# Later weight conversions, a sum's guard on ScalarE, four score buffers and transposes two slots behind, in an attention and two-layer-block kernel

## The chip, the cores and the metric

The kernel runs on one core of a Trainium2 chip. The metric is device time in microseconds (us) for one execution, median of three runs. The engines are named as in the profile: PE is TensorE (PEld its weight loads), DVE is VectorE, ACT is ScalarE, POOL is GpSimd, SP is SyncE, which issues all DMAs here.

## What is computed

The reference chains three parts. Inputs are float32 activations and weights drawn in float64.

```python
scores = scale * q @ k.T + decay           # decay from cumulated log f, causal mask
attn = exp(scores - max); attn = attn / (attn.sum() + 1e-9)
x = (attn @ v)  as (2304 tokens, 512)      # 4 batches x 8 heads, 576 tokens, head size 64
h = x @ w_in;  g = h * tanh(softplus(h));  y = g @ w_out      # 512 -> 2048 -> 512
a = y @ w1; b = y @ w2; out = ((a * b) @ w3) @ w_out2         # 512 -> 1024 -> 1024 -> 512
```

The weights w_in, w_out, w1, w2, w3 and w_out2 come as float64 bit patterns and are converted to float32 on the chip. Nearly every product is made of three matmuls over a high and a low part of its operands (float32r), so each tensor is split into two tiles.

## The kernel before, in words

The program has two phases. Phase A holds attention for 16 pairs of heads, all weight conversions, the product of w3 and w_out2 (`wp_unit`), and the first layer (`l1_all`) for batches 0 to 2. Phase B holds the first layer of batch 3 and then everything behind it, in eight blocks of 288 tokens.

Attention is cut into units. A unit is 128 rows of one head's scores; a pair of heads has 9 units, of which the last (number 8 of the pair) takes the 64 remaining rows of both heads and reads all 576 columns. There are 144 units. The loop in `phase_a` has a slot for each unit and seven more. In slot s it writes out, in program text:

- `scores(s)`: two to eight matmuls on PE into one of two PSUM banks, ps_s (L391, L392, L401);
- `softmax_a(s)`: masking and row minimum on DVE into a buffer P (L415; L417 and L418 for a pair's last unit), then the exponential on ACT in place, with the row sum (L419);
- `transposes(s - T_LAG)`: up to five PE transposes of P into ps_t, two PSUM banks (L455), a copy of the high part to `pt` on ACT (L483) and a subtraction for the low part on DVE (L485);
- `inv_sums` on a pair's last slot: 1e-9 is added to nine row sums (L426), and the reciprocal is taken (L427), both on DVE. `inv_rows` transposes it (L434, L436) and stores it to DRAM, `inv_load` reads it back broadcast as R, and `x_parts` multiplies by it (L521);
- `pv` in two slots of each pair: attention times v into ps_v (L503), then `x_rows` on ACT and DVE (L515, L516), `x_parts` on POOL and ACT;
- filler: matmuls of `wp_unit` (L550) or of the first layer (L580), a planned number for each slot.

A conversion is a DMA of 512 KB (L111) into one of two buffers `cvr`, a scaling on POOL (L124; for other weights on ACT, L126) and three bit operations on DVE (L134, L135, L136). For w_out (tiles `cvu`, 16 of them) and for w1 and w2 (tiles `cvv`, 16) the result is stored to DRAM (L143) for phase B. The loop places job i of these 32 in slot `W_OUT_SLOT + int(W_OUT_STEP * i)`.

The program's text does not fix the order on an engine. A scheduler gives each engine its instructions by priority and by its own model of when each could run; the score, transpose and subtraction steps have a raised priority, the conversions do not. Each engine then runs its list in that order.

Of the kernel before, what the change touches and what calls it, by code (L numbers as in the profile page):

```python
# [8 lines left out]
F32 = mybir.dt.float32  # L9
# [3 lines left out]
AF = mybir.ActivationFunctionType  # L13
ALU = mybir.AluOpType
# [4 lines left out]
B, H, S, D = 4, 8, 576, 64  # L19
# [11 lines left out]
PT_N = 1536  # L31

QK_AT = ((-2, 4, 5, 5, 6), (3, 9, 9, 10, 11))
T_LAG = 1
PV_AT = (3, 5)
HB = 3
CV = 2
# [6 lines left out]
MID = 7  # L44
EARLY = 10
W3_STEP = 2.25
W_OUT_STEP = 2.25
PRE = 6
WP_END = 51
W_IN_SLOT = 34  # L50
W_IN_STEP = 1.25
W_OUT_SLOT = 62
L1_S = (42, 75, 114, 153)

MM_PAIRS = ((0, 0), (0, 1), (1, 0))
# [12 lines left out]
class Kernel:  # L68
# [116 lines left out]
    def att_pool(self):  # L185
        nc = self.nc
        self.attp = self.tc.tile_pool(name="att", bufs=1)
        a = self.att = self.attp.__enter__()
        self.psp = self.tc.tile_pool(name="psa", bufs=1, space=PSUM)
        p = self.psp.__enter__()  # L190
        self.ps_s = [p.tile([128, 512], F32, name=f"ps_s{i}") for i in range(2)]
        self.ps_t = [p.tile([128, 512], F32, name=f"ps_t{i}") for i in range(2)]
        self.ps_v = p.tile([128, 1024], F32, name="ps_v")
        self.ident = a.tile([128, 128], F32, name="ident")
        self.m1 = a.tile([128, 512], BF16, name="m1")
        self.m4 = a.tile([128, TB], BF16, name="m4")
        self.pt = a.tile([128, 6 * PT_N + 3 * 64], F32R, name="pt")
        self.pt4 = self.pt[:, 6 * PT_N:]
        self.TT = [a.tile([128, 2, 1216], F32R, name=f"T{i}") for i in range(3)]
        self.T = [(t[:, 0], t[:, 1]) for t in self.TT]  # L200
        self.P = [a.tile([128, n], F32, name=f"P{i}") for i, n in enumerate((512, 512, S))]


    def decay_log(self):
# [67 lines left out]
    def zeros(self):  # L272

        nc = self.nc
        z = self.m1[:, :384]
        nc.gpsimd.memset(self.P[2][0:4], 1.0)
        for i in (0, 2, 1):
# [8 lines left out]
            for c in (d0, d0 + S):  # L286
                nc.scalar.copy(t2[0:4, c:c + S], self.P[2][0:4])

# [115 lines left out]
    def softmax_a(self, u):  # L404
        _, _, c = self.unit(u)
        nc = self.nc
        n = S if c == 4 else 128 * (c + 1)
        P = self.P[u % 3]
        i = (0, 1, 2, 3, 5, 6, 7, 8, 4)[u % 9]
        if u % 9 == 0:  # L410
            self.sums = self.att.tile([128, 16], F32, name=f"sum{u // 9}", tag="sum", bufs=2)
        st = self.sums[:, 9 + u % 3:10 + u % 3]
        ttr = nc.vector.tensor_tensor_reduce
        if c < 4:
            ttr(P[:, :n], self.ps_s[u % 9 % 2][:, :n], self.m1[:, 512 - n:], -0.125, 3.0e38, ALU.add, ALU.min, st)  # L415
        else:
            ttr(P[:, :TB], self.ps_s[0][:, :TB], self.m1[:, :TB], -0.125, 3.0e38, ALU.add, ALU.min, self.sums[:, 12:13])  # L417
            ttr(P[:, TB:n], self.ps_s[1][:, :TB], self.m4, -0.125, self.sums[:, 12:13], ALU.add, ALU.min, st)  # L418
        nc.scalar.activation(P[:, :n], P[:, :n], AF.Exp, bias=st, scale=-1.0,  # L419
                             accum_out=self.sums[:, i:i + 1])  # L420

    def inv_sums(self):

        nc = self.nc
        r = self.sums[:, 0:9]
        nc.vector.tensor_scalar(r, r, 1e-9, None, ALU.add)  # L426
        nc.vector.reciprocal(r, r)  # L427
        self.inv = r

# [18 lines left out]

    def transposes(self, u):
        _, _, c = self.unit(u)  # L450
        P = self.P[u % 3]
        for kc in range(c + 1):
            o = 128 * (kc % 4)
            k = 64 if kc == 4 else 128
            self.nc.tensor.transpose(self.t_bank(u, kc)[0:k, o:o + 128], P[:, 128 * kc:128 * kc + k], self.ident)  # L455
# [190 lines left out]
    def phase_a(self):  # L646
# [48 lines left out]
        def job(s, key, src, fin, *a):  # L695
            at(s, self.cv_load, key, src)
            conv.setdefault(s + 1, []).append(key)
            at(s + 2, fin, *a)
# [7 lines left out]
        for i in range(32):  # L706
# [3 lines left out]
            else:  # L710
                key, src, dst = f"v{f}", self.cols((self.w1, self.w2)[f % 2], f // 2), self.w12_scr
            job(W_OUT_SLOT + int(W_OUT_STEP * i), key, src, self.cv_store, key, dst[f])
        for p in range(NPAIR):
# [21 lines left out]
        for s in range(nslot + 7):  # L735
# [3 lines left out]
            with self.tc.high_priority(offset=HP_ATT):  # L739
                if s < nslot:  # L740
                    self.scores(s)
                if 0 <= s - T_LAG < nslot:
                    self.transposes(s - T_LAG)
                    self.pt_parts(s - T_LAG, False)
            for key in conv.get(s, []):
# [5 lines left out]
            self.run_filler(k)  # L751
            if 0 <= s - T_LAG < nslot:
                with self.tc.high_priority(offset=HP_ATT):
                    self.pt_parts(s - T_LAG, True)
            for key in conv.get(s, []):
# [287 lines left out]
```

## Time and profile before

| quantity | value |
|---|---|
| median of 3 runs | 1089.82 us (1088.87 to 1092.64) |
| the profiled execution's own time | 1095.71 us |
| its span, first to last instruction | 1094.0 us |
| PE busy | 980.8 us, 90% |
| DVE, ACT, POOL busy | 788.5, 639.1, 592.7 us |
| mean granted TensorE clock | 0.954 of full speed |

The span is the time between the first and the last instruction of one profiled execution; a busy share is an average over both phases. The last score unit's exponential starts at 488.0 us, and phase B's first matmuls follow at about 505 us. The granted clock has two levels, 1.2 and 2.4 GHz, shown as 0.50 and 1.00 where a stretch has one level alone.

### The profile page before, as it was taken

To read this page: it belongs to the slowest core of one execution; us is meant where nothing else is said; L and a number is where in the kernel's file an instruction comes from. 1 tells how busy PE (TensorE), PEld (TensorE's weight loads), DVE (VectorE), ACT (ScalarE), POOL (GpSimd) and SP (SyncE) were. 2 spreads that over 40 slices of the span, in tenths; PEclk is the share of its full clock that TensorE was granted. 3 is DMA by queue.
4 is the path that set the end of the run, shared out by engine and by line. 5 is a ranking of instruction groups with operands and counts; after the bars stand their busy time and mean duration, and the time that the engine had idled before them with its cause. 6 is when DMAs were issued, how large, how long until landed. Compare 5 with 4: busy or idle time off the path is not lost. (4 is left out here: it accounts for less than half of the span.)

```text
span 1094.0 us, 20534 instructions
## 1 busy us (share of the span) xinstructions
PE 980.8 (90%) x6784; PEld 935.2 (85%) x6784; DVE 788.5 (72%) x1800; ACT 639.1 (58%) x1660; POOL 592.7 (54%) x690
## 2 busy tenths in 40 slices
PE   0797778888789888998979999999999999999998
PEld 0576657788789878998878999999999999999998
DVE  7977788785666776643897886868868687886821
ACT  7676778876665677764666454545545454454511
POOL 5956677775666677623685453534545353453500
PEclk9898869899889998998999999999999999999999
DMA  7865457667667867425864111121111112111100
GB/s 212 207 209 173 131 164 219 195 183 222 199 201 229 249 203 219 150 72 170 298 188 126 39 44 45 44 61 39 50 45 44 50 44 61 39 50 40 27 23 22
DMA packets 107086, 136.37 MB, mean 125 GB/s; under 512 B 11092, under 2 KB 83172, under 8 KB 106980
## 3 DMA queue, kind: packets, MB, share of 16 engines
q1 hardware_dynamic: 106980, 135.07, 41.7%
q8 instruction: 53, 0.87, 0.3%
q14 instruction: 53, 0.43, 0.1%
HBM read 98.39 MB, written 36.54 MB: 123 GB/s over the span
## 5 line engine op out<-in xcount | busy, mean ns | idle before, releaser
L580 PE MATMUL ps_l<-x,wi 128*128 128x288 f32 x1536 | 250.6, 312 | 14.5 <-ACT x L88 4.1
L580 PEld LDWEIGHTS ps_l<-x,wi 128*128 128x128 f32 x1536 | 224.7, 198 | 20.5 <-ACT hst L587 5.2
L889 PE MATMUL ps_x<-g,wo 128*128 128x288 f32 x1536 | 224.5, 297 | 6.8 <-POOL g L102 3.7
L889 PEld LDWEIGHTS ps_x<-g,wo 128*128 128x128 f32 x1536 | 209.6, 189 | 11.0 <-POOL g L102 6.0
L102 POOL TENSOR_TENSOR g<-mb,g 128x288 fp32r<-128x288 f32 x128 | 111.5, 871 | 135.5 <-ACT g L88 130.7
L102 POOL TENSOR_TENSOR T<-raw,T 64x288 fp32r<-64x288 f32 x128 | 113.3, 904 | 16.9 <-ACT T L339 11.9
L88 ACT CAST g<-mb 128x288 fp32r<-128x288 f32 x128 | 55.3, 432 | 112.8 <-DVE mb L853 82.5
L830 ACT ACTIVATE ma<-ma 128x288 f32<-128x288 f32 x128 | 56.6, 442 | 101.9 <-DVE ma L826 101.9
L908 PE MATMUL ps_y<-x,w 128*128 128x288 f32 x768 | 108.2, 296 | 2.6 <-ACT x L897 1.3
L908 PE MATMUL ps_l<-x,w 128*128 128x288 f32 x768 | 108.1, 295 | 0.0
L908 PEld LDWEIGHTS ps_y<-x,w 128*128 128x128 f32 x768 | 104.0, 189 | 3.0 <-ACT x L897 1.5
L908 PEld LDWEIGHTS ps_l<-x,w 128*128 128x128 f32 x768 | 104.3, 189 | 0.0
L455 PE MATMUL ps_t<-ident,P 128*128 128x128 f32 (+1 forms) x400 | 73.0, 301 | 32.9 <-DVE pt L485 32.5
L419 ACT ACTIVATE P<-P,sum 128x512 f32<-128x512 f32 (+2 forms) x144 | 85.4, 595 | 27.8 <-DVE sum L415 24.9
L485 DVE TENSOR_TENSOR pt<-ps_t,pt 128x128 fp32r<-128x128 f32 (+2 forms) x288 | 83.2, 331 | 24.6 <-ACT pt L483 24.1
L834 DVE SCALAR_TENSOR_TENSOR mb<-ma 128x288 f32<-128x288 f32 x128 | 63.3, 494 | 51.0 <-POOL g L102 49.2
L849 POOL TENSOR_TENSOR mb<-mb,hl 128x288 f32<-128x288 f32 x64 | 63.4, 991 | 62.7 <-DVE cs L847 29.3
L849 POOL TENSOR_TENSOR mb<-mb,hsp 128x288 f32<-128x288 f32 x64 | 61.8, 965 | 64.1 <-issue 25.7
L483 ACT CAST pt<-ps_t 128x128 fp32r<-128x128 f32 (+2 forms) x288 | 73.0, 314 | 34.5 <-PE ps_t L455 32.6
L848 DVE SCALAR_TENSOR_TENSOR ma<-cs,ma 128x288 f32<-128x288 f32 x128 | 89.5, 699 | 2.4
L455 PEld LDWEIGHTS ps_t<-ident,P 128*128 128x128 f32 (+1 forms) x400 | 52.3, 152 | 41.9 <-DVE pt L485 34.0
L847 DVE SCALAR_TENSOR_TENSOR cs<-mb,ma 128x288 f32<-128x288 f32 x128 | 73.6, 575 | 13.4 <-ACT ma L839 12.6
(123 smaller groups left out, 1917.7 us busy)
## 6 DMA issues: line engine op xcount, KB each, us to landing
raw<-in_qk_dram SPq DMA_DIRECT2D x64, 288.0 KB
h_scr<-h SPq DMA_DIRECT2D x96, 144.0 KB
hl<-h_scr SPq DMA_DIRECT2D x64, 144.0 KB
hsp<-h_scr SPq DMA_DIRECT2D x64, 144.0 KB
cvrt<-in_w3t_dram SPq DMA_DIRECT2D x16, 512.0 KB
cvri<-in_w_in_dram SPq DMA_DIRECT2D x16, 512.0 KB
cvru<-in_w_out_dram SPq DMA_DIRECT2D x16, 512.0 KB
cvrv<-in_w_dram SPq DMA_DIRECT2D x16, 512.0 KB
```

Source lines behind the costliest of these rows:

```text
L102: self.nc.gpsimd.tensor_tensor(lo[..., c], raw[..., c], f32(hi[..., c]), ALU.subtract)
L419: nc.scalar.activation(P[:, :n], P[:, :n], AF.Exp, bias=st, scale=-1.0, accum_out=self.sums[:, i:i + 1])
L455: self.nc.tensor.transpose(self.t_bank(u, kc)[0:k, o:o + 128], P[:, 128 * kc:128 * kc + k], self.ident)
L483: nc.scalar.copy(hi, a)
L485: nc.vector.tensor_tensor(self.pt_dst(hd, 1, k, 128 * c, w), a, f32(hi), ALU.subtract)
L580: mm(o[:, :TB], w, x, start=i == 0, stop=i == 11)
L834: self.nc.vector.scalar_tensor_tensor(b, a, 2.0, a, ALU.add, ALU.mult)
L847: nc.vector.scalar_tensor_tensor(e, b, 2.0, a, ALU.add, ALU.mult)
L848: nc.vector.scalar_tensor_tensor(a, e, 2.0, a, ALU.subtract, ALU.mult)
L849: nc.gpsimd.tensor_tensor(b, b, self.hl[c], ALU.mult)
L889: mm(self.xb(e), self.wo[f][:, 512 * a + 128 * e:512 * a + 128 * e + 128], g[:, TB * b:TB * b + TB], start=f == 0 and k == 0, stop=f == 15 ...
L908: mm(ps, self.w12[f, i][:, 512 * a + 128 * e:512 * a + 128 * e + 128], self.x2[e][:, TB * b:TB * b + TB], start=n == 0, stop=n == 11)
```

## The change

Five edits. `T_LAG` goes from 1 to 2, so a unit is transposed two slots behind its scores. There are four P buffers, each 576 columns wide, in place of three of 512, 512 and 576. The 32 conversion jobs of w_out, w1 and w2 are placed from slot 88 in steps of 1.9 slots, in place of slot 62 and 2.25. The addition of 1e-9 is an ACT instruction.

```diff
-T_LAG = 1
+T_LAG = 2
...
-W_OUT_STEP = 2.25
+W_OUT_STEP = 1.9
...
-W_OUT_SLOT = 62
+W_OUT_SLOT = 88
...
-        self.P = [a.tile([128, n], F32, name=f"P{i}") for i, n in enumerate((512, 512, S))]
+        self.P = [a.tile([128, S], F32, name=f"P{i}") for i in range(4)]
...
-        P = self.P[u % 3]
+        P = self.P[u % 4]
...
-        nc.vector.tensor_scalar(r, r, 1e-9, None, ALU.add)
+        nc.scalar.activation(r, r, AF.Copy, bias=1e-9)
         nc.vector.reciprocal(r, r)
```

What the scheduler makes of it is seen in the order of instructions. Three places follow.

The first place is DVE, the last of the 32 conversions (`cvv15`). `sum14` and `sum15` are the row sums of pairs 14 and 15 (units 126 to 134 and 135 to 143), and L415 is the row-minimum step of a unit. Before:

```order
L415 ISA P0_92,sum14_4750<-ps_s1_81,m1_86 128x512
L415 ISA sum14_4750 128x1
L134 TENSOR_SCALAR cvv15_4966<-cvv15_4966 128x512
L485 TENSOR_TENSOR pt_88<-ps_t1_83,pt_88 128x128
L135 SCALAR_TENSOR_TENSOR cvv15_4966<-cvrv15_4932,cvv15_4966 128x512
L136 SCALAR_TENSOR_TENSOR cvv15_4966<-cvrv15_4932,cvv15_4966 128x512
```

Of the change:

```order
L415 ISA P3_95,sum15_4996<-ps_s0_80,m1_86 128x128
L415 ISA sum15_4996 128x1
L485 TENSOR_TENSOR pt_88<-ps_t1_83,pt_88 128x128
L134 TENSOR_SCALAR cvv15_5415<-cvv15_5415 128x512
L135 SCALAR_TENSOR_TENSOR cvv15_5415<-cvrv15_5397,cvv15_5415 128x512
L485 TENSOR_TENSOR pt_88<-ps_t0_82,pt_88 64x64 x2
L136 SCALAR_TENSOR_TENSOR cvv15_5415<-cvrv15_5397,cvv15_5415 128x512
```

The last conversion moved from behind the row minimum of unit 129 to behind that of unit 139. The first one (`cvu0`) stands behind that of unit 59 before and of unit 58 in the change, although its slot number is 26 higher.

The second place is DVE at the end of pair 9. The rows `128x2x64 x4` and `64x64 x2` are the six subtractions of the pair's last unit, number 89; `sum10` belongs to the next pair. Before:

```order
L427 RECIPROCAL sum9_3067<-sum9_3067 128x9
L485 TENSOR_TENSOR pt_88<-ps_t0_82,pt_88 128x2x128 x2
L415 ISA P2_94,sum10_3407<-ps_s0_80,m1_86 128x384
L415 ISA sum10_3407 128x1
L485 TENSOR_TENSOR pt_88<-ps_t1_83,pt_88 128x2x64 x4
L485 TENSOR_TENSOR pt_88<-ps_t0_82,pt_88 64x64 x2
L134 TENSOR_SCALAR cvu15_3629<-cvu15_3629 128x512
```

Of the change:

```order
L415 ISA P1_93,sum10_3295<-ps_s1_81,m1_86 128x512
L415 ISA sum10_3295 128x1
L485 TENSOR_TENSOR pt_88<-ps_t1_83,pt_88 128x2x64 x4
L415 ISA P2_94,sum10_3295<-ps_s0_80,m1_86 128x128
L415 ISA sum10_3295 128x1
L485 TENSOR_TENSOR pt_88<-ps_t1_83,pt_88 128x128
L134 TENSOR_SCALAR cvu13_4177<-cvu13_4177 128x512
L485 TENSOR_TENSOR pt_88<-ps_t0_82,pt_88 64x64 x2
```

The row minima run one unit further ahead of unit 89's subtractions, and a conversion's first step now stands ahead of the last two of them.

The third place is PE at the end of phase A. L434 transposes the last pair's reciprocals, L503 is `pv`, and the tiles x12 to x15 are inputs of the first layer for batch 3 (x15 belongs to the last pair). Before:

```order
L434 MATMUL ps_t0_82<-ident_85,sum15_5072 9x128
L580 MATMUL ps_l1_65<-x14_0_5246,wi0_1343 128x288 x2
L580 MATMUL ps_l0_64<-x12_1_4627,wi0_1343 128x288 x3
L580 MATMUL ps_l0_64<-x13_1_4958,wi0_1343 128x288 x3
L580 MATMUL ps_l0_64<-x14_1_5250,wi0_1343 128x288 x3
L503 MATMUL ps_v_84<-pt_88,V15_5296 128x256 x2
L503 MATMUL ps_v_84<-pt_88,V15_5296 128x128 x2
L503 MATMUL ps_v_84<-pt_88,V15_5296 128x320 x6
L503 MATMUL ps_v_84<-pt_88,V15_5296 128x192 x2
L503 MATMUL ps_v_84<-pt_88,V15_5296 128x64
L580 MATMUL ps_l1_65<-x15_0_5487,wi0_1343 128x288
```

Of the change, from L434 on:

```order
L434 MATMUL ps_t0_82<-ident_85,sum15_4996 9x128
L503 MATMUL ps_v_84<-pt_88,V15_5262 128x320 x5
L503 MATMUL ps_v_84<-pt_88,V15_5262 128x192 x2
L580 MATMUL ps_l1_65<-x8_1_3179,wi12_1932 128x288 x3
L580 MATMUL ps_l1_65<-x9_1_3520,wi12_1932 128x288 x3
L580 MATMUL ps_l1_65<-x10_1_3863,wi12_1932 128x288 x3
```

And of the change, around the last `pv`:

```order
L503 MATMUL ps_v_84<-pt_88,V15_5262 128x320 x6
L503 MATMUL ps_v_84<-pt_88,V15_5262 128x192 x2
L503 MATMUL ps_v_84<-pt_88,V15_5262 128x64
L580 MATMUL ps_l0_64<-x12_1_4544,wi0_1327 128x288 x3
L580 MATMUL ps_l0_64<-x13_1_4884,wi0_1327 128x288 x3
L580 MATMUL ps_l0_64<-x14_1_5211,wi0_1327 128x288 x3
L580 MATMUL ps_l1_65<-x15_0_5488,wi0_1327 128x288
```

The transpose of the reciprocals moved ahead of 55 matmuls of the first layer that stood ahead of it, and nine matmuls that stood ahead of the last `pv` now stand between it and the first matmul that needs x15.

## Rows read from the trace of the kernel before

**Rows 1.** The page: span, and PE's busy time.

```profile
span 1094.0 us, 20534 instructions
...
PE 980.8 (90%) x6784; PEld 935.2 (85%) x6784; DVE 788.5 (72%) x1800; ACT 639.1 (58%) x1660; POOL 592.7 (54%) x690
```

**Rows 2.** Busy time by stretch: start:end, length, engines, granted clock, DMA share, GB/s.

```profile
35.00:211.00 176.00, 142.74 (x750) 118.20 (x749) 142.99 (x339) 134.76 (x349) 126.02 (x146) 0.87 0.63 179
211.00:360.00 149.00, 127.78 (x860) 119.98 (x861) 100.88 (x275) 99.30 (x284) 100.95 (x121) 0.91 0.70 208
360.00:442.00 82.00, 72.34 (x501) 68.69 (x500) 57.71 (x161) 56.47 (x164) 59.00 (x71) 0.94 0.73 217
442.00:501.00 59.00, 59.00 (x449) 58.24 (x448) 29.64 (x99) 37.55 (x120) 19.48 (x25) 1.00 0.32 103
...
600.00:1094.00 494.00, 487.55 (x3644) 484.29 (x3644) 355.71 (x774) 228.38 (x564) 200.20 (x222) 1.00 0.15 43
```

**Rows 3.** PE's waits from 35 to 510 us: total us, times, longest.

```profile
PE ps_t L455 <- DVE pt L485: 32.5, 19, 4.0
PE ps_s L391 <- DVE sum L417: 6.2, 7, 3.5
```

**Rows 4.** DVE in order of time, 265 to 272 us: start, length, idle before.

```profile
266.94 0.69 DVE L136 SCALAR_TENSOR_TENSOR cvu<-cvru,cvu 128x512 int32<-128x512 int32 x1
269.21 1.01 DVE L134 TENSOR_SCALAR cvu<-cvu 128x512 int32<-128x512 int32 x1 [1.57 <-POOL cvu L124]
270.14 0.41 DVE L485 TENSOR_TENSOR pt<-ps_t,pt 128x256 fp32r<-128x256 f32 x1
```

**Rows 5.** POOL in order of time in the same stretch.

```profile
267.24 1.93 POOL L124 TENSOR_SCALAR cvu<-cvru 128x256 f32<-128x256 f32 x2 [1.84 <-DMA cvru<-in_w_out_dram]
```

**Rows 6.** PE in order of time: five stops at ends of pairs.

```profile
240.59 0.66 PE L455 MATMUL ps_t<-ident,P 128*128 128x128 f32 x4 [1.92 <-DVE pt L485]
...
270.60 0.69 PE L455 MATMUL ps_t<-ident,P 128*128 128x128 f32 x2 [3.74 <-DVE pt L485]
...
297.72 1.12 PE L455 MATMUL ps_t<-ident,P 128*128 128x128 f32 x4 [3.69 <-DVE pt L485]
...
326.08 0.58 PE L391 MATMUL ps_s<-T 128*128 128x256 f32 x1 [3.49 <-DVE sum L417]
...
414.83 0.90 PE L455 MATMUL ps_t<-ident,P 128*128 128x128 f32 x3 [4.00 <-DVE pt L485]
```

**Rows 7.** Busy time by stretch, behind three stops: columns as in rows 2.

```profile
240.60:247.00 6.40, 6.40 (x49) 6.16 (x49) 4.69 (x19) 4.35 (x19) 6.19 (x9) 1.00 0.58 167
270.10:276.90 6.80, 6.30 (x25) 5.92 (x26) 4.44 (x14) 2.02 (x7) 6.51 (x8) 0.50 0.75 240
505.60:512.40 6.80, 6.45 (x25) 6.12 (x26) 1.30 (x2) 3.49 (x8) 3.08 (x5) 0.50 0.61 173
```

**Rows 8.** ACT, DVE, POOL and PE in order of time at phase A's end.

```profile
501.48 0.63 ACT L515 COPY xx<-ps_v 64x576 f32<-64x576 f32 x1 [2.46 <-PE ps_v L503]
...
502.14 0.75 DVE L516 TENSOR_TENSOR xx<-ps_v,xx 64x576 f32<-64x576 f32 x1 [2.62 <-ACT xx L515]
...
503.89 1.54 POOL L521 TENSOR_TENSOR xx<-xx,R 128x288 f32<-128x288 f32 x2 [16.73 <-DMA R<-inv_scr]
...
505.20 0.40 PE L580 MATMUL ps_l<-x,wi 128*128 128x288 f32 x1 [3.75 <-ACT x L88]
```

**Rows 9.** The chain that ended last, 843 to 870 us: start, length, count.

```profile
843.85 1.75 PE ps_x L889 x11
845.59 1.59 PE ps_y L928 x12
```

**Rows 10.** The added step's line and a small ACT copy: ns min/median/max, first and last start.

```profile
L426 DVE TENSOR_SCALAR sum<-sum x16: 173/728/820, 59.2 to 488.9; 128x9 f32<-128x9 f32 x16
...
L436 ACT COPY inv<-ps_t x16: 238/255/257, 74.4 to 498.8; 9x128 f32<-9x128 f32 x16
```

**Rows 11.** DVE's waits from 35 to 505 us: total us, times, longest.

```profile
DVE P L415 <- PE ps_t L455: 22.2, 26, 3.0
```

**Rows 12.** First-layer matmuls (L580) by stretch: length, PE, PEld, clock, DMA.

```profile
272.00:297.00 25.00, 10.74 (x56) 9.88 (x56) 0.90 0.71 207
360.00:391.00 31.00, 19.83 (x127) 17.90 (x126) 0.98 0.79 237
391.00:414.00 23.00, 6.79 (x39) 5.75 (x38) 0.95 0.70 202
```

More of the change, by code (lines that the diff above doesn't have):

```diff
@@ L450, in transposes @@
         _, _, c = self.unit(u)
-        P = self.P[u % 3]
+        P = self.P[u % 4]
         for kc in range(c + 1):
```

## The prediction, made before the changed kernel ran

> **What bounds the kernel now.** I began with the page: PE is busy for 980.8 of 1094.0 us [rows 1], so at most 113 us of the span is not PE's, and the question is where it lies. The view of busy time by stretch says so [rows 2]. From 600 us on PE works 487.55 of 494 us at a granted clock of 1.00. From 442 to 501 us it works the whole 59 us, also at 1.00. The loss is in phase A before that: 33.3 us idle from 35 to 211 us (176 less 142.74), 21.2 us from 211 to 360 and 9.7 us from 360 to 442, and in these stretches the clock is 0.87, 0.91 and 0.94. The first layer of batch 3 and all behind it stand in the same order in both kernels, so whatever changes must change ahead of about 510 us.
>
> The list of waits then says what PE waits for [rows 3]: 32.5 us in 19 waits is one thing, a transpose waiting for the subtraction (L485) that frees its PSUM bank. The timeline of one such stop shows why the subtraction is late. At 267.6 us DVE has finished a conversion's last step, and the next instruction in its order is the first step (L134) of the next conversion. It idles 1.57 us until POOL has scaled that weight, runs L134 for 1.01 us, and only then comes the subtraction at 270.14 us [rows 4]. POOL in turn had waited 1.84 us for the weight's DMA [rows 5]. So one late load stops POOL, then DVE, which takes its instructions in order, then PE. There are five such stops at ends of pairs in the stretch where w_out, w1 and w2 are converted: 1.92, 3.74, 3.69, 3.49 and 4.00 us, 16.84 in all [rows 6].
>
> A stop costs more than its length. Behind the stop of 3.74 us the clock was 0.50 for 6.8 us, in which PE was busy for 6.30 us; the stretches behind the three other long ones read alike, at 0.50 for 6.7 to 6.8 us. Behind the stop of 1.92 us it stayed at 1.00 [rows 7]. Half of 6.8 us, 3.4 us, is the most that such a stretch takes from PE.
>
> Last, the seam of the phases. The last `pv` ends at 501.45 us (505.20 less 3.75), ACT and DVE add its halves until 502.89 us, but POOL's multiplication by R starts only at 503.89 us, when the DMA of R has landed. PE stands for 3.75 us until 505.20 us [rows 8], and from 505.6 to 512.4 us its clock is 0.50 [rows 7].
>
> **The change part by part.** The sum is made against the profiled execution's 1095.71 us, 5.9 us over the median of 1089.82; I take the difference over to the median unchanged.
>
> *Conversions.* The slot numbers say 26 slots later; the order of instructions says otherwise. The first conversion of w_out stands behind unit 58's row minimum (before: 59), the last behind unit 139's (before: 129). The scheduler takes a conversion as soon as a buffer is free, so what changes is that 32 conversions are spread over 81 units in place of 70. No instruction or byte is added or removed. Price: the idle 21.2 and 9.7 us, plus the clock's share. A clock of 0.91 over 149 us is 26.8 us at half speed, one of 0.94 over 82 us is 9.8 us; half of 36.6 is 18.3 us [rows 2]. That makes 49.2 us. Behind the last of the five stops, at 414.83 us [rows 6], hardly any of it falls; it lies at about unit 118, and behind that 5 of the 32 conversions stand before, 8 in the change. Were the whole loss due to the other 27, each would cost 1.8 us, and three moved into the quiet part would give 5.5 us. At the other end nothing, if the loss goes along with them. Not all of the loss is theirs, so I take 3 us.
>
> *The seam.* Two things move on PE. The transpose of the last pair's reciprocals (L434) is 55 matmuls earlier, so R's way through DRAM, which ended 1.0 us after the sums it is multiplied with (503.89 against 502.89), is hidden. And nine matmuls now stand behind the last `pv`: at 1.59 us for 12 [rows 9] they fill 1.2 us. The stop shrinks from 3.75 to about 1.55 us, which gives 2.2 us. A stop of 1.55 us lies under that of 1.92 us which left the clock at 1.00 [rows 7], but one such row is little evidence, so I count half of the 3.4 us: 1.7. Together 3.9 us; the bounds are 1.0 (only R's lateness) and 5.6.
>
> *The addition on ACT.* On DVE the step took 173 to 820 ns with a median of 728; a copy of the same small size on ACT took 255 [rows 10]. Sixteen times 0.73 us of DVE, 11.6 us, go away and 16 times 0.26 us, 4.1 us, come to ACT, with the reciprocal now waiting on ACT; behind it in DVE's order stand a unit's subtractions, but the order puts it behind later score steps, so ACT should be done. DVE's time matters only where PE waits for DVE: 32.5 of 475 us [rows 3], 7%, so 0.8 us of 11.6. I take 1 us; the bounds are nothing and 11.6. On this the Trainium skill disagrees, in "ScalarE: Activation LUTs", section "Rules for kernel authors": it sends an add to VectorE, and budgets about 0.3 us per ACTIVATE plus 0.83 ns per element, an estimate of 4.9 us on ScalarE for the sixteen. By the page this edit should give nothing; the sum would end 1 us later. The row of 728 ns says that here VectorE is the dearer place.
>
> *Four buffers and a lag of two.* DVE waited 22.2 us, 26 times, for a transpose to free P [rows 11]. With three buffers and lag 1 a buffer is free two slots before it is needed, with four and lag 2 also two; and the chain on PE's path, from one unit's subtraction to the next transposes into the same bank, keeps its length. So I expect no gain; at most 19 us, the 32.5 us of [rows 3] less the 13.35 of the four such stops in [rows 6]. A cost is visible: x of a batch's last pair is ready one unit later, and at the start of batches 1 and 2 PE has little else. In the stretches around these starts it had 56 and 39 first-layer matmuls, against 127 in a full one [rows 12]. A unit there takes 23/9, 2.6 us, so up to 5.1 us for two; the filler still left hides most, and I take 1 us.
>
> The sum: 3 + 3.9 + 1 less 1 is 7 us. 1095.71 becomes 1088.7, and the median 1083.
>
> **The rivals.**
>
> *Slower: the conversions get in the way of the last unit of a pair.* Between the row minimum of a pair's last unit and the last of that unit's six subtractions, pairs 6 to 14, DVE's order has 8 first steps of conversions before and 12 in the change; the four more stand ahead of the last two subtractions, as shown for pair 9. The transposes of the next pair's second unit need that bank. The price of one from the stops: 16.84/8 is 2.1 us, and four of the five had a clock at half behind them at up to 3.4 us, 13.6/8 is 1.7 us, together 3.8. Four make 15 us; less the 4 us of the seam the time is 11 us up, 1101. Against it: up to the first four subtractions the count falls from 8 to 6, and the last two are needed one unit later. It decides the sign from about two such stops on.
>
> *No change.* The conversions behave as before, wherever they stand, and the seam gains only 1 us because the sums take R's place and the clock falls all the same: 1089.
>
> *Much faster.* DVE, freed of 11.6 us and with conversions thinned from one per 2.2 units to one per 2.5, is late at few pair ends. A third of the 49.2 us, 16 us, gives 1074. For it speaks that from 442 to 501 us, with one conversion left, PE lost nothing; against it that the early part, where PE idled 33.3 us, has as many conversions as before.
>
> **How the numbers follow.** Chances: the forecast (1079 to 1087) 0.4, much faster 0.14, no change 0.18, slower 0.28. A change of 0.3%, 3.3 us, is about what three runs of this kernel can tell from none. Faster by more than that is the first two cases: 0.53 (a little of the forecast's lower end is taken off). The same is the third and that rest: 0.2. Slower is 0.27. The range for 8 in 10 reaches from 1071, past which a few of the much faster cases lie, to 1099, which holds three of four extra stops. The forecast's own range is 1079 to 1087.
>
> **What the changed profile would show.** Right: R's wait at the seam is gone from POOL's list, the stop ahead of the first matmul with x15 is under 2 us, and the clock after it is 1.00. The added step is some 0.25 us on ACT with no wait of the reciprocal for it. PE's waits for L485 stay near 32 us; those between 211 and 442 us fall by a fifth. Wrong: stops behind L134 at the transposes of a pair's second unit (the slower rival); a new stop between 442 and 501 us, where six conversions now stand in place of one, which at 4.0 us and a slow clock would cost 7.4 us; or stops that fall in the early part, from 35 to 211 us, which I left unpriced.

## The result and the profile after

The changed kernel takes 1100.96 us (median of 8 runs, 1097.75 to 1107.24) against 1090.41 us of the kernel before beside it (8 runs, 1088.87 to 1094.8). The ratio is 1.0097, 95% interval [1.0072, 1.0122]: 10.5 us slower. The prediction said 1083, and its range ended at 1099.

The page of the changed kernel, for its profiled execution of 1097.83 us:

```profile
span 1096.0 us, 20419 instructions
...
PE 983.2 (90%) x6784; PEld 928.0 (85%) x6784; DVE 775.2 (71%) x1784; ACT 639.7 (58%) x1676; POOL 596.0 (54%) x690
```

The span is only 2.0 us longer than that of [rows 1], since those came from one of the slowest runs of the kernel before (1095.71), these from one of the fastest of the change. Both were therefore profiled once more: `before_again` took 1088.84 us (span 1087.1), `after_again` 1100.54 (span 1098.8). Where the two pairs differ in what matters, I give both.

Busy time by stretch after the change, columns as in [rows 2]:

```profile
35.00:211.00 176.00, 140.05 (x705) 113.79 (x703) 131.65 (x325) 128.04 (x337) 119.90 (x138) 0.84 0.61 174
211.00:360.00 149.00, 131.90 (x900) 119.38 (x900) 99.57 (x282) 107.98 (x315) 107.55 (x128) 0.97 0.67 197
360.00:442.00 82.00, 71.60 (x473) 66.00 (x472) 51.71 (x150) 55.16 (x161) 53.10 (x64) 0.90 0.74 217
442.00:501.00 59.00, 57.78 (x439) 56.54 (x438) 35.63 (x98) 36.18 (x113) 27.71 (x33) 1.00 0.44 144
600.00:1094.00 494.00, 488.22 (x3648) 484.70 (x3648) 357.69 (x776) 230.12 (x570) 202.34 (x223) 1.00 0.15 43
```

Phase B is what it was. In phase A, PE handles 45 matmuls fewer up to 211 us than in [rows 2] (705 against 750), catches 40 of them up by 360 us, and falls behind again by 28 up to 442 us (473 against 501). The catching up is not borne out by the later pair: there PE falls behind by 43, 14 and 42 matmuls in these three stretches.

The waits of PE from 35 to 510 us:

```profile
PE ps_t L455 <- DVE pt L485: 17.2, 15, 2.7
PE ps_s L391 <- POOL T L102: 7.0, 8, 2.2
PE ps_l L580 <- ACT h L587: 6.4, 7, 1.5
PE ps_s L391 <- DVE sum L415: 5.5, 12, 1.1
```

The wait that led [rows 3] with 32.5 us has almost halved (33.8 and 14.8 us in the later pair), and yet the kernel is slower. Smaller waits of other kinds stand in its place.

The seam of the phases, PE and POOL in order of time:

```profile
504.26 1.75 PE L503 MATMUL ps_v<-pt,V 128*128 128x256 f32 x13
505.85 1.43 PE L580 MATMUL ps_l<-x,wi 128*128 128x288 f32 x9
508.91 0.40 PE L580 MATMUL ps_l<-x,wi 128*128 128x288 f32 x1 [1.63 <-ACT x L88]
...
507.60 1.54 POOL L521 TENSOR_TENSOR xx<-xx,R 128x288 f32<-128x288 f32 x2 [15.42 <-DMA vr<-w_scr]
```

The stop ahead of the first matmul with x15 is 1.63 us where [rows 8] had 3.75, with nine matmuls ahead of it, as forecast. The last sum of ACT and DVE ends at 507.47 us, and POOL starts 0.13 us later, so it is this sum that releases POOL, as the row of `after_again` below says, and not the DMA named in the row above. The clock at this place:

```profile
501.00:510.00 9.00, 7.02 (x52) 6.47 (x50) 1.50 (x2) 2.93 (x6) 2.40 (x4) 1.00 0.39 133
510.00:520.00 10.00, 8.76 (x53) 8.28 (x53) 3.94 (x7) 6.15 (x15) 3.55 (x5) 0.83 0.78 252
```

It holds at 1.00 through the stop. Behind it 1.7 of 10 us are lost, which is 3.4 us at half speed, where [rows 7] had 6.8 us.

How late all of this comes is read from POOL's last multiplication by R, which makes x15. The rows of `before_again`, of `after_again` and of the experiment with the later conversions alone (`conv_alone`, below):

```profile
497.95 1.54 POOL L521 TENSOR_TENSOR xx<-xx,R 128x288 f32<-128x288 f32 x2 [16.86 <-DMA R<-inv_scr]
```

```profile
510.20 1.54 POOL L521 TENSOR_TENSOR xx<-xx,R 128x288 f32<-128x288 f32 x2 [15.44 <-DVE xx L516]
```

```profile
495.68 1.54 POOL L521 TENSOR_TENSOR xx<-xx,R 128x288 f32<-128x288 f32 x2 [16.72 <-DMA R<-inv_scr]
```

From this start to the end of the span there are 589.2 us before (1087.1 less 497.95) and 588.6 after; in the first pair of profiles 590.1 and 588.4. So everything behind it is 0.6 to 1.7 us shorter, and the whole loss was made earlier: 3.7 us in the first pair, 12.3 us in the later one. The same stretch takes 587.0 us in `conv_alone`, which has the old seam (1082.7 less 495.68), so a gain of this size is not clear of what two orders differ by.

### The profile page after: what moved, and what is told of

The parts are those of the page before. It is cut to its first block, busy times and chain, and to the rows that moved or that the text cites. A ratio compares the mean times of both kernels' runs of the same rounds, so it can differ in the third digit from the quotient of the medians.

```text
span 1096.0 us, 20419 instructions
## 1 busy us (share of the span) xinstructions
PE 983.2 (90%) x6784; PEld 928.0 (85%) x6784; DVE 775.2 (71%) x1784; ACT 639.7 (58%) x1676; POOL 596.0 (54%) x690
## 5 line engine op out<-in xcount | busy, mean ns | idle before, releaser
L580 PE MATMUL ps_l<-x,wi 128*128 128x288 f32 x1536 | 244.4, 306 | 17.1 <-ACT h L587 6.4
L580 PEld LDWEIGHTS ps_l<-x,wi 128*128 128x128 f32 x1536 | 218.0, 193 | 26.0 <-ACT h L587 9.8
L102 POOL TENSOR_TENSOR T<-raw,T 64x288 fp32r<-64x288 f32 x128 | 109.6, 875 | 24.2 <-ACT T L339 19.8
L485 DVE TENSOR_TENSOR pt<-ps_t,pt 128x128 fp32r<-128x128 f32 (+2 forms) x288 | 84.8, 331 | 35.6 <-ACT pt L483 34.9
L415 DVE CUSTOM_DVE_ANT_0 P<-ps_s,m 128x384 f32<-128x384 f32 (+3 forms) x128 | 61.1, 482 | 49.9 <-PE ps_t L455 40.3
L419 ACT ACTIVATE P<-P,sum 128x128 f32<-128x128 f32 (+3 forms) x144 | 85.4, 594 | 17.8 <-DVE sum L415 17.0
L455 PE MATMUL ps_t<-ident,P 128*128 128x128 f32 (+1 forms) x400 | 75.4, 298 | 18.9 <-DVE pt L485 17.2
L503 PE MATMUL ps_v<-pt,V 128*128 128x320 f32 (+4 forms) x416 | 77.8, 311 | 12.2 <-ACT pt L483 4.5
```

Source lines behind the costliest of these rows:

```text
L102: self.nc.gpsimd.tensor_tensor(lo[..., c], raw[..., c], f32(hi[..., c]), ALU.subtract)
L485: nc.vector.tensor_tensor(self.pt_dst(hd, 1, k, 128 * c, w), a, f32(hi), ALU.subtract)
L503: mm(ps[:, base + q:base + q + w], V[:, kc, :], rhs, start=i == 0, stop=i == n - 1)
L580: mm(o[:, :TB], w, x, start=i == 0, stop=i == 11)
```

## The experiments

All times are medians. The ratio is against the kernel before on the same chip, which had medians from 1089.3 to 1090.4 there; it is an estimate from all runs and can differ a little from the ratio of the medians. A loss in us in the text is the ratio's share of that median.

| run | what differs from the kernel before | us | ratio [95%] |
|---|---|---|---|
| `lag_alone` | lag of two | 1102.31 | 1.0134 [1.0103, 1.0164] |
| `buffers_alone` | four P buffers | 1101.86 | 1.0098 [1.0062, 1.0134] |
| `add_alone` | addition on ACT | 1096.52 | 1.0061 [1.0037, 1.0085] |
| `conv_alone` | later conversions | 1083.23 | 0.9940 [0.9921, 0.9959] |
| `lag_and_buffers` | lag of two, four P buffers | 1103.13 | 1.0133 [1.0102, 1.0164] |
| `conv_and_add` | later conversions, addition on ACT | 1098.81 | 1.0081 [1.0055, 1.0107] |
| `all_but_lag` | all but the lag | 1097.97 | 1.0084 [1.0052, 1.0116] |
| `edits_to_unit_53` | lag, buffers, addition in pairs 0 to 5 | 1102.33 | 1.0122 [1.0098, 1.0145] |
| `edits_from_unit_54` | all five edits, in pairs 6 to 15 | 1098.08 | 1.0086 [1.0066, 1.0106] |
| `prio_high` | HP_ATT 200 | 1089.24 | 0.9991 [0.9974, 1.0007] |
| `prio_none_with_lag` | lag, buffers, HP_ATT 0 | 1100.88 | 1.0110 [1.0079, 1.0141] |
| `reorder_pv` | HP_PV 60 | 1099.42 | 1.0074 [1.0045, 1.0103] |
| `reorder_w3` | W3_STEP 2.3 | 1095.43 | 1.0060 [1.0041, 1.0080] |
| `reorder_att` | HP_ATT 30 | 1097.07 | 1.0070 [1.0045, 1.0095] |
| `after_reorder_w3` | all five edits, W3_STEP 2.3 | 1101.16 | 1.0109 [1.0079, 1.0139] |
| `after_reorder_att` | all five edits, HP_ATT 30 | 1111.68 | 1.0201 [1.0172, 1.0230] |

**One part at a time.** The edits are lines of the diff above, taken alone or together.

`lag_alone`: 

> The kernel before with the lag of two slots alone: three P buffers of 512, 512 and 576 columns, the old conversion slots, the addition on DVE. Theory A, that score work is pulled ahead of the filler matmuls without the attention getting done any earlier: of the 1728 filler matmuls of the first phase and of batch 3's first layer, PE's order has 1108 ahead of pair 15's first scores in place of 1200, and 92 at 0.132 us make it 12 us slower than before, near 1102. Theory B, that conversions stand ahead of the last subtractions of a pair's last unit: the count for pairs 6 to 14 is 7 in place of 8, so it is not slower, 1086 to 1091.

`conv_alone`: 

> The kernel before with the conversions' slot and step alone (88 and 1.9). Theory A: 1212 filler matmuls stand ahead of pair 15's scores in place of 1200, so no change, 1087 to 1091. Theory B: 10 conversions stand ahead of the last subtractions in place of 8, 7.6 us slower by the price of 3.8 us for each, near 1098.

`lag_and_buffers`: 

> The kernel before with the lag of two and the four P buffers, with the old conversion slots and the addition on DVE. Theory A: 1116 filler matmuls ahead of pair 15's scores, as in the whole change, so 11 us slower, near 1101, and the whole change's cost is in these two edits. Theory B: 10 conversions ahead of the last subtractions in place of 8, near 1098, and less slow than the whole change with its 12.

`all_but_lag`: 

> The whole change without the lag: four P buffers, the new conversion slots, the addition on ACT, transposes one slot behind. Theory A: 1114 filler matmuls ahead of pair 15's scores, since with four buffers the scores can run one unit further ahead anyhow; 11 us slower than before, near 1101. Theory B: 11 conversions ahead of the last subtractions, near 1101 as well. If it is near 1090, the lag itself is the cause in a way that neither count shows.

The lag alone costs more than the whole change, and without the lag most of the loss stays. The conversions alone make the kernel 6.5 us faster than before (0.006 of 1089.5), beyond the bound of 5.5, and faster than both kernels. They gain where the prediction looked for it. `conv_alone` by stretch:

```profile
35.00:211.00 176.00, 144.64 (x754) 119.83 (x752) 140.09 (x337) 135.24 (x348) 128.77 (x148) 0.85 0.63 180
...
360.00:442.00 82.00, 74.22 (x539) 71.54 (x538) 54.69 (x160) 58.00 (x166) 58.52 (x69) 0.98 0.76 228
```

PE gets through 539 matmuls from 360 to 442 us, where [rows 2] has 501 (505 in `before_again`), and the clock is 0.98 in place of 0.94 (0.96). Theory B, which counts heads of conversions ahead of the last subtractions, falls: 7 of them go with a loss of 14.6 us in `lag_alone` (0.0134), 10 with a gain here.

**Filler and priority.** PE's order in the change has 1116 first-layer matmuls ahead of the first scores of pair 15, before it has 1200. Theory A priced each one held back at 0.132 us. A higher or lower priority of the attention steps shifts that number without touching the edits.

```diff
-HP_ATT = 100
+HP_ATT = 200
```

`prio_high`: 

> The kernel before, with none of the five edits, but the raised priority of scores, transposes and subtractions (HP_ATT) at 200 in place of 100. PE's order is as before up to pair 13, and behind that 1140 filler matmuls stand ahead of pair 15's scores in place of 1200; conversions and their place on DVE hardly move (8 ahead of the last subtractions, as before). Theory A, filler held back behind attention work that comes no earlier: 60 matmuls at 0.132 us, 8 us slower, near 1097. Theory C, that the lag and the buffers cost by a later x at the batches' starts and in the early pairs: not slower than 1092, since those are untouched.

`prio_none_with_lag`: 

> The lag of two and four P buffers as in the change (conversion slots and addition as before), with HP_ATT at 0, which lets filler go earlier: 1164 filler matmuls ahead of pair 15's scores against 1116 with HP_ATT 100. Theory A: 36 held back, 4.8 us slower than the kernel before, near 1094, so 8 us faster than lag and buffers with HP_ATT 100 (1103.1). Theory C: the lag stays and so does its cost, 1100 to 1105.

`conv_and_add`: 

> The change without its lag and without the fourth P buffer: new conversion slots and the addition on ACT. Theory A: 1233 filler matmuls ahead of pair 15's scores in place of 1200, 4 us faster than before, near 1085. Theory C: no cost either, 1083 to 1089. If it is near 1100, neither the lag nor the buffers are the cause.

`buffers_alone`: 

> The kernel before with four P buffers of 576 columns alone, transposes one slot behind. Theory A: 1173 filler matmuls ahead of pair 15's scores, 3.6 us slower, near 1093. Theory C: the row minima run one unit further ahead, as with the lag, and the early pairs (3 to 5) take some 5 to 10 us longer, near 1098.

Theory A falls three times: `prio_high` with 1140 such matmuls should have lost 8 us and lost none; `conv_and_add` with 1233 should have gained and lost 8.8; `prio_none_with_lag` has 1164 and loses 12. That lag or buffers cost by themselves (theory C) can't be all either, since `conv_and_add` has neither. The buffers did not do what they are for: DVE's waits for a P buffer in `buffers_alone`, from 35 to 505 us, against 22.2 us in 26 times in [rows 11]:

```profile
DVE P L415 <- PE ps_t L455: 29.8, 25, 3.1
```

**Where in phase A.** At the start of the first layer the slow kernels share a mark. The stretches from 176 to 200 and from 300 to 420 us in `before_again`:

```profile
176.00:200.00 24.00, 21.91 (x161) 20.75 (x160) 19.77 (x47) 19.04 (x56) 17.06 (x20) 1.00 0.73 221
300.00:420.00 120.00, 103.99 (x735) 98.56 (x734) 82.62 (x223) 79.10 (x227) 84.22 (x98) 0.95 0.74 222
```

and in `after_again`:

```profile
176.00:200.00 24.00, 19.69 (x110) 16.91 (x111) 15.30 (x39) 15.33 (x48) 14.55 (x18) 0.79 0.68 201
300.00:420.00 120.00, 105.03 (x698) 97.67 (x697) 75.31 (x214) 80.68 (x241) 75.66 (x90) 0.90 0.67 196
```

After the change PE does 110 matmuls where it did 161. From 170 to 181 us it is busy for 6.51 us, before for 8.49; the rest goes in many short stops, of which these are four (`after_again`, PE in order of time):

```profile
173.41 0.44 PE L391 MATMUL ps_s<-T 128*128 128x384 f32 x1 [0.74 <-DVE sum L415]
...
174.68 0.50 PE L391 MATMUL ps_s<-T 128*128 128x512 f32 x1 [0.65 <-DVE sum L415]
...
176.10 0.54 PE L580 MATMUL ps_l<-x,wi 128*128 128x288 f32 x1 [0.69 <-ACT x L88]
...
181.05 0.58 PE L391 MATMUL ps_s<-T 128*128 128x256 f32 x1 [1.65 <-POOL T L102]
```

```profile
170.00:181.00 11.00, 6.51 (x30) 4.04 (x28) 8.58 (x22) 10.90 (x28) 10.71 (x15) 0.78 0.58 174
176.20:186.40 10.20, 7.55 (x27) 5.91 (x28) 6.60 (x19) 7.78 (x26) 9.18 (x11) 0.50 0.64 182
```

No stop is as long as those of [rows 6], and still the clock is 0.50 from 176.2 us on for 10.2 us (the second row of busy time by stretch). Theory D put the loss here. To test it, the edits were made in one half of the pairs only:

```diff
-T_LAG = 1
+T_SPLIT = 54
...
+        return [u for u in (s - 2, s - 1) if 0 <= u < 9 * NPAIR and u + (1 if u < T_SPLIT else 2) == s]
...
-        nc.vector.tensor_scalar(r, r, 1e-9, None, ALU.add)
+        if False if p < T_SPLIT // 9 else True:
+            nc.scalar.activation(r, r, AF.Copy, bias=1e-9)
+        else:
+            nc.vector.tensor_scalar(r, r, 1e-9, None, ALU.add)
```

`edits_from_unit_54`: 

> All five edits, but lag, buffer choice and addition only from unit 54 (pair 6) on; the order on PE is that of the kernel before up to its instruction 766, so past the start of the first layer at 176 to 200 us. Theory D, that the cost is made at the start of the first layer, where every slow variant so far had a cluster of stops and a clock at half between 179 and 195 us that the kernel before, conversions alone and the higher priority do not have: no such window, 115 us of matmul work done by 200 us as before, and a time of 1083 to 1092. Theory A or C, that lag and buffers cost wherever they are: 7 to 10 us slower than before, 1096 to 1100.

`edits_to_unit_53`: 

> Lag of two, four buffers and the addition on ACT up to unit 53 alone, behind that as before; old conversion slots. Theory D: the window of a half clock between 179 and 195 us is there, some 7 us of matmul work are missing at 200 us, and the time is 1096 to 1102. Theory A or C: a third of the units have the edits, so 3 to 5 us slower, 1092 to 1095.

(In `edits_to_unit_53` the low part of unit 53 is computed from transposes that are overwritten by then; all other work is that of the kernel.) `before_again` and `after_again` ran beside these two:

`before_again`: 

> The kernel before once more, for a second profile. Theory D: 115 us of matmul work done at 200 us and a full clock from 168 to 210 us again; the five stops at ends of pairs between 238 and 415 us need not come back at the same places, since they hang on when loads land.

`after_again`: 

> The changed kernel once more, for a second profile. Theory D: a half clock between 179 and 195 us again, and 107 to 109 us of matmul work done at 200 us. If the window is gone, the theory rests on chance.

The rows of `edits_from_unit_54`:

```profile
176.00:200.00 24.00, 21.21 (x154) 19.80 (x153) 19.12 (x45) 19.20 (x54) 16.78 (x20) 1.00 0.71 209
300.00:420.00 120.00, 105.15 (x693) 98.17 (x694) 77.51 (x222) 78.82 (x228) 81.64 (x96) 0.89 0.70 208
```

Its first layer starts as before, and it loses 9.4 us (0.0086) all the same, later. Each half alone costs about as much as the whole (9.4 and 13.3 us against 10.5). D falls as the cause: the mark is real, but a kernel without it ends as late.

**The order itself.** What `conv_alone` and `prio_high` share with the kernel before is the start of PE's order. Counted in the 6784 matmuls of each trace, `conv_alone` leaves it after the 1072nd, `prio_high` after the 784th and `edits_from_unit_54` after the 766th; every other kernel leaves it between the 39th and the 282nd. (The expectations count rows of the scheduler's list in place of matmuls.) Theory E: that order is a good one by chance, and drawing it up afresh costs. Three edits change neither an instruction nor a buffer nor an engine, but the order; the counts of instructions on PE, DVE, ACT and POOL stay those of [rows 1]:

```diff
-HP_PV = 50
+HP_PV = 60
```

```diff
-W3_STEP = 2.25
+W3_STEP = 2.3
```

```diff
-HP_ATT = 100
+HP_ATT = 30
```

`add_alone`: 

> Before, with 1e-9 added on ACT and nothing else. By the prediction this gains 1 us (bounds 0 and 11.6). Theory E (the order of instructions in the kernel before is a good one by chance, and any edit that makes the scheduler draw it up afresh loses 8 to 13 us): 1098 to 1103. Theory F (each edit costs something by itself): the addition was dear on top of the conversions, +15.6 us from conv_alone to conv_and_add, so 1100 to 1105 here too; this run alone does not tell E from F, it tells both from the prediction's 1088.

`reorder_pv`: 

> Before, with the priority of the pv steps at 60 in place of 50. No instruction, buffer, engine or slot changes, only the order that the scheduler draws up, on PE from the 120th row on (the first transposes of reciprocals). Theory E: slower all the same, 1098 to 1103. Theory F (the edits themselves cost): as before, 1087 to 1092.

`reorder_w3`: 

> Before, with W3_STEP at 2.3 in place of 2.25: a few conversions of w3 (all in the first 33 slots) are placed one slot later, nothing else changes, but the order on PE is drawn up afresh from the 225th row on. Theory E: 1098 to 1103. Theory F: 1087 to 1092.

`reorder_att`: 

> Before, with the priority of scores, transposes and subtractions at 30 in place of 100; at 200 it made no difference (1089.24), but there the order on PE stayed the same up to the 565th row, here it leaves it at the 73rd. Theory E: 1098 to 1103. Theory F: 1087 to 1092.

All three lose, 6.5 to 8.1 us by their ratios of 1.0060 to 1.0074. That is less than E's 8 to 13 us, but theory F, by which only the edits themselves cost, expected no loss. `prio_high` is a fourth re-ordering of this kind, and it loses nothing (0.9991): it leaves the order of before later than the three. The early mark is there too. `reorder_pv` by stretch and its leading wait on PE (35 to 510 us):

```profile
176.00:200.00 24.00, 19.73 (x112) 16.98 (x113) 18.09 (x47) 19.55 (x51) 19.99 (x25) 0.86 0.64 187
```

```profile
PE ps_t L455 <- DVE pt L485: 21.8, 17, 4.5
```

The same with the edits in:

`after_reorder_w3`: 

> The changed kernel with W3_STEP at 2.3 in place of 2.25, the edit of reorder_w3: only the order is drawn up afresh, on PE from the 168th row on. Three orders without the edits came to 1095.4 to 1099.4, one order with all five to 1100.96. If the five edits cost nothing by themselves, this draw falls among the three: 1095 to 1100. If they cost the 3 to 4 us that part the change from the mean of the three: 1099 to 1104. If the order of the changed kernel was itself an unlucky one: under 1095.

`after_reorder_att`: 

> The changed kernel with the priority of scores, transposes and subtractions at 30 in place of 100, the edit of reorder_att; the order on PE leaves that of the change at the 53rd row. As for after_reorder_w3: 1095 to 1100 if the edits cost nothing by themselves, 1099 to 1104 if they cost 3 to 4 us, under 1095 if the changed kernel's own order was an unlucky one.

Three orders with all five edits have ratios of 1.0097, 1.0109 and 1.0201, three without any 1.0060, 1.0070 and 1.0074. So about 7 us go with a new order alone, where it is new from early on. The edits add to it: against the mean of the latter, 1.0068, 3 to 5 us in two draws and 14 in the third. With three draws each, the share of the edits has no sharper figure. That the order of before is good by chance is not shown: if its settings were once picked for their time, most re-orderings would lose in the same way, and no run here tells the two apart.

**Not the clock alone.** Between `before_again` and `after_again` the mean granted clock from 35 to 510 us goes from 0.93 to 0.90, while PE's idle time falls from 69.8 to 63.8 us (475 less the busy time):

```profile
35.00:510.00 475.00, 405.20 (x2611) 366.55 (x2610) 333.82 (x877) 334.69 (x928) 313.71 (x369) 0.93 0.63 189
```

```profile
35.00:510.00 475.00, 411.18 (x2556) 365.09 (x2555) 319.96 (x855) 329.60 (x928) 308.30 (x360) 0.90 0.62 184
```

That reads as if the clock were the cause. One profile can mislead here: that of `before_again` had a mean clock of 0.965, above every one of 72 timed runs of the kernel before (at most 0.964). Over these 72 the mean clock is 0.9573 and the loss by it, (1 - clock) times the span, 46.4 us; over 8 of the change 0.9554 and 49.1 us. Of 11.5 us between the mean spans (1087.9 and 1099.4) the clock takes 2.7. (This measure counts idle stretches at the low clock too, so it is rough.)

Taken against the kernel before on the same chip, the timed runs part the two causes. In `reorder_w3` and `reorder_att` the clock is not lower than before (0.9585 and 0.9583 against 0.9566), and in `reorder_pv` the loss by it is larger by 1.3 of the 8.9 us between the mean spans: little or nothing of what a new order costs is the clock. In the kernels that have the lag or the four buffers throughout or from unit 54 on, the loss by the clock is 4.7 to 8.3 us larger than before (`lag_alone` 5.3, `buffers_alone` 6.3, `edits_from_unit_54` 7.9); in `conv_and_add` and `add_alone`, which have neither, 1.3 and 2.3, and in `edits_to_unit_53`, which has them up to unit 53 alone, 0.6. So what these two edits add goes at least in part with a lower clock. How they lower it is not shown, and over the 8 runs of the change itself the figure is the smaller 2.7.

## Why the prediction was wrong

**The step that failed** is "Four buffers and a lag of two": "I take 1 us", with a cost bound of 5.1. Alone they measure 14.5 us (1.0133). The cost named was x of a batch's last pair coming later, sized as one unit of 2.6 us on an otherwise unchanged order. The last multiplication for batch 2 is indeed later, by 4.3 us in the first pair of profiles (411.8 against 407.5) and by 14.0 in the later one (414.1 against 400.1); but it is at 404.3 to 410.0 us in the three re-orderings too, which have the old lag. The premise of an unchanged order is what failed: the scheduler drew up a new one, and PE's order leaves that of before after 39 matmuls. Each edit was priced as if the rest stayed, and three edits that leave all prices alone still lose about 7 us. The other half of the 14.5 goes with the lag and the buffers; by the rough measure above 6.2 us of it are the clock's, which the prediction did not price for this edit.

**The addition.** "I take 1 us" of gain was wrong in sign: `add_alone` loses 6.6 us (0.0061), as much as a neutral re-ordering, so no cost of its own is shown either. The price of the step was near: the added step of the change, nanoseconds min/median/max,

```profile
L426 ACT ACTIVATE sum<-sum x16: 195/210/257, 58.9 to 489.7; 128x9 f32<-128x9 f32 x16
```

against a forecast of 255, and the reciprocal waited for it once, for 0.8 us. By the rule of the Trainium skill that the prediction weighed ("ScalarE: Activation LUTs", "Rules for kernel authors"), which sends an add to VectorE, the edit gains nothing, and no run shows a gain; as one instruction the step is shorter on ACT all the same, 0.21 against 0.73 us. The 0.3 us per instruction that the prediction took from there is given for a bias read from an operand, and the bias here is a constant.

**The seam** was right in its mechanism: R is no longer waited for, and the stop is 1.63 us (forecast 1.55). For the clock the prediction took half of 3.4 us as even odds between a full fall and none, and named 1.00 behind the stop as the sign of being right; the clock fell for half as long, 0.83 over 10 us, so that the 1.7 us came true is luck. What the seam gave is smaller than 3.9 us: 0.6 to 1.7 us behind the start of the last multiplication, and some 0.9 us ahead of it, since this start follows the end of the last `pv` by 1.59 us (507.60 less 504.26 and 1.75) and no more by 2.44 (503.89 less 501.45).

**The conversions** were right alone in sign and place, between 360 and 442 us, and too small in size: they gain 6.5 us where I took 3, with a bound of 5.5. On a re-drawn order it is not kept: `conv_and_add` has a ratio of 1.0081, `add_alone` 1.0061.

**The rivals.** The slower one gave 1101, the measured time, by luck: its mechanism did not happen, since PE's waits for L485 should have grown by four stops and went from 32.5 to 17.2 us. The forecast's own sign, waits near 32 us that fall by a fifth between 211 and 442 us, failed as well: there they went from 15.3 to 6.3 us. One of its signs of being wrong did show: the early part, from 35 to 211 us, which it left unpriced, is where PE falls behind by 45 matmuls (43 in the later pair). The clue that was passed over stands in [rows 3]: PE's leading wait was taken for what bounds phase A. It is 26.4 to 33.8 us in the four kernels' profiles that were not slower (`before`, `before_again`, `conv_alone`, `prio_high`), and 9.4 to 24.1 in all the slower ones but `edits_to_unit_53` (28.5), whose second half has the old lag and buffers. PE's idle time up to the last multiplication is 62 to 76 us in all of them, so a high value says that much of it lies in this one wait; it is no price of what a better order would give.

**What stays open** is which feature of the order of before makes it good. From 35 us to the start of the multiplication that makes x15, the traces of before, of the change and of the three neutral re-orderings hold 2556 to 2563 matmuls, and PE's idle time is 64 to 68 us in all of them. The difference stands in PE's busy time: 402.3 and 395.2 us in the two profiles of before, 403.6 to 406.7 in the re-orderings, 407.6 and 411.2 in those of the change. The two profiles of before have the same order and differ by 7 us, as much as is to be explained, so one profile of each kernel can't part it further, and no single place was found that decides.

## What to carry to other kernels

Where a scheduler sets the order, an edit is first a new draw of the whole order: run several neutral re-orderings, of the kernel before and of the change, and compare the edit with their spread before giving it a cause. Price edits from the old trace only where the order stays, as it did at the start for the conversions; and don't take the longest list of waits for the bound, since a re-ordering can halve it and lose time. One profile of each kernel can also mislead by nearly the whole effect (the first pair's spans differ by 2.0 us, the timed runs by 10.5): look at the clock and the span of all timed runs beside it.

## What the hardware showed beyond that

The small addition on DVE took 173 to 820 ns [rows 10], and when it ended went with POOL. DVE and POOL in order of time in the kernel before:

```profile
122.83 2.46 POOL L102 TENSOR_TENSOR x<-xx,x 128x288 fp32r<-128x288 f32 x2
...
124.55 0.77 DVE L426 TENSOR_SCALAR sum<-sum 128x9 f32<-128x9 f32 x1
...
488.87 0.17 DVE L426 TENSOR_SCALAR sum<-sum 128x9 f32<-128x9 f32 x1 [0.94 <-ACT P L419]
```

The one at 124.55 us ends 0.03 us behind POOL's instruction (125.32 against 125.29); the one at 488.87 us, with POOL idle, takes 0.17 us. Fifteen of the sixteen end 0.03 or 0.04 us behind the end of a POOL instruction. This agrees with the Trainium skill, "SBUF — State Buffer", section "Summary: rules for kernel authors": if DVE is in its two-port mode, or has two inputs in SBUF while the GpSimd instruction reads SBUF, the second of the two to issue is blocked until the first finishes. That this step, with its one input, ran in the two-port mode is not shown by any run. On ACT the same step is steady at 195 to 257 ns.
